# Dividing the attention weights on VectorE instead of GpSimd, in a fused attention + SwiGLU + GELU kernel

## The chip, the cores and the metric

The kernel runs on one core of one Trainium2 chip. The metric is device time in microseconds (us) of one execution; lower is better. Engines are named as the profile names them: PE is TensorE (PEld its weight loads), DVE is VectorE, ACT is ScalarE, POOL is GpSimd (Pool in the prose), SP is the queue that issues the DMAs.

## What is computed

Attention with 4 batches of 8 heads, 576 positions and 64 columns a head, a causal mask and a bias from cumulative sums; then a SwiGLU layer (512 to 1536 to 512) with an RMS norm ahead of it, then a GELU-like layer (512 to 2048 to 512), over 2304 tokens, all in float32:

```python
scores = scale * q @ k.T;  cum = cumsum(maximum(s, 0))
scores = where(causal, -1e9, scores + minimum(-(cum_i - cum_j), 0))
scores = scores - max(scores)
attn = exp(scores)
attn = attn / (sum(attn) + 1e-09)
x = attn @ v
x = swiglu(x / rms(x) * rms_g)
return (h * sigmoid(1.702 * h)) @ w_out,  with h = x @ w_in
```

The change concerns the line that divides by the sum.

## The kernel before, in words

Phase A is the attention, one head after another, 32 in all. The 576 queries of a head are cut into blocks of 64, 128, 128, 128 and 128; under the causal mask these have 64, 192, 320, 448 and 576 keys, so that the weights P of a head are five tiles with 1600 columns together (the first two share one tile, `p01`). For a head, in this order:

- `scores` (L298): PE multiplies into PSUM (L307, or L309 and L310 from head 8 on); DVE adds the mask and takes the row minimum while it copies to SBUF (L323, a custom instruction with an accumulator read behind it).
- `expo` (L329): ACT takes the exponential in place and the row sums SU (L333).
- `recip` (L338): ACT adds 1e-9 to the sums (L340), DVE inverts them into RC (L341), one instruction of five columns a head.
- `norm` (L343): five `tensor_scalar` instructions multiply the five tiles by their column of RC in place (L348). The engine is `en("NORM", ...)`, a letter of a ten-letter string: before, all are `g`, Pool.
- `transp` (L362): PE transposes P into PSUM (L368; the first block of a head L370). In heads 0 to 11 the result is copied out by ACT or DVE (L104, L106); from head 12 on ACT writes a rounded part (L378) and DVE the rest of it (L379, `ptl`).
- `pv` (L397): PE multiplies with V (L416 or L427), ACT and DVE put the result into `xT` (L104; L432, L437).

Ahead of that stands the preparation of q, k and v, which splits a number into a rounded part and its rest (`rnd`, L98 and L100; `rest`, L111 on Pool and L113 on DVE), and in the same stretch the first twelve weight units are decoded from 64-bit floats by `load_unit` (L134): DMA into `wst` (two buffers), then ACT L155, DVE L156, Pool L157, DVE L158 and L160, Pool L162, ACT L98, Pool L164.

From head 13 on the SwiGLU layer's first four column blocks are worked as filler between the heads (`fa_gv`, `fa_act`, `fa_out`: PE L171 and L530, DVE L513, L514 and L113). Phase B (L613, from about 408 us) does the rest of both layers; PE is busy almost throughout there, and no norm lies in it.

The order of the work on each engine is not written out: each call gets a key in heads (`at(key, fn, ...)`, L178; the norms of head h have h + 1.0 to h + 1.08, `recip` h + 0.95), an offset per kind (`off`), and from that a priority. A scheduler with a timeline of its own takes the calls by priority and readiness and fixes one in-order list of instructions for each engine when the kernel is built. P has three buffers a tile (`PPB`), the two PSUM pools for scores and transposes two each.

Of the kernel before, what the change touches and what calls it, by code (L numbers as in the profile page):

```python
# [30 lines left out]
E_MAX = 122880.0 - 2.0 ** -7  # L31


PRM = {'RF': set(), 'QF': {0, 1, 2, 3, 4, 5, 6, 7}, 'VF': {0, 1, 2, 3, 4, 5, 6, 7, 8, 9, 10, 11}, 'DEC0': 7.7, 'DEC1': 12.54, 'DADD': 'ggggggggg', 'DLO': 'ggggvgggg', 'QA': 'ss', 'KA': 'gs', 'VH': 'vg', 'VL': 'gg', 'NORM': 'gggggggggg', 'F0': 13.06, 'F1': 34.62, 'off': {'fa_split': 2.82, 'fa_out': 1.98, 'prep_k': 2.88, 'prep_v32': 0, 'norm': -1.96, 'prep_v': 0.11, 'fa_gv': 0.29, 'prep_load': 0.68, 'prep_f32': 0, 'prep_cum': 0.22, 'scores': -0.04, 'recip': 0, 'transp': -0.26, 'rms_mean': 0, 'load_unit': 0, 'rms_apply': 0, 'expo': 0, 'rms_sq': -1.1, 'pv': 0.19, 'prep_q': 2.7, 'rcast': -0.77}, 'QL': 'gv', 'KL': 'gg', 'PTC': 'ssvv', 'XC': 'ss', 'RMA': 'ggvvgvggvvgv', 'XH': 'sssssvs', 'XL': 'vgggggg', 'HH': 'ssg', 'YO': 'ssssvvs', 'T0': 1.5, 'NX': 7, 'SX': 3, 'TX': 2, 'VX': 2, 'PPB': 3, 'PTB': 5, 'QKB': 2, 'G0': 4, 'XHB': 2, 'VB': 2, 'HHB': 5, 'GA': 4, 'AJ': [0, 1, 2, 3, 4, 5, 6], 'LATE': 1, 'PLB': 4, 'EJ': 2, 'EL': 3}


@with_exitstack
def attention_then_swiglu_then_gelu(ctx: ExitStack, tc, qT, kT, vp, s, w1, w2, gT, out):
# [21 lines left out]
    NIN = len(TIN)  # L60
    GA, G0 = PRM["GA"], PRM["G0"]
    AJ = []
    for t in PRM["AJ"]:
        AJ.append((t, list(range(GA))) if t < 10 else (t - 10, list(range(GA, G0))))
    TA = sum(n for _, n in TIN)
    NW = 3 * G0
    NSLOT = 16
    QF = PRM["QF"]
    VF = PRM["VF"]
    RF = PRM["RF"]  # L70

# [20 lines left out]
    def en(name, i=0):  # L92
        v = PRM[name]
        return ENG[v[i % len(v)]]
# [727 lines left out]
```

## Time and profile before

| | |
|---|---|
| median of 3 runs | 1132.45 us (1128.24 to 1134.29) |
| profiled execution, its own time | 1130.19 us |
| its span, first to last instruction | 1128.4 us |
| mean granted TensorE clock | 0.973 of full speed |
| PE busy | 1087.4 us (96%) |
| DVE busy | 741.9 us (66%) |
| ACT busy | 531.2 us (47%) |
| POOL busy | 443.0 us (39%) |
| the five norms of 32 heads, POOL L348 | 160 instructions, 88.9 us |

Busy is time inside instructions; an instruction that started and then had to wait inside for a port counts as busy, so its length is compared with the shortest of its kind. A page line "idle before, releaser" tells how long an engine had nothing to do before such an instruction, and what ended that. PE's time is that of the whole program; the attention ends about 368 us after the start.

### The profile page before, as it was taken

The page shows a single profiled execution, that of the slowest core. Times are in us where ns is not written, and L with a number is a line of the kernel's source. Part 1 is how long each engine was busy: PE and PEld are TensorE (multiplying, and loading weights), DVE is VectorE, ACT ScalarE, POOL GpSimd, SP SyncE. Part 2 cuts the span into 40 slices and gives each one's busy share as a digit, 9 for nine tenths or more (in the row PEclk, how much of TensorE's full clock was granted, in tenths as well). Part 3 has the DMA queues.
Part 4 walks back from the last instruction along what each step waited for, and adds up shares of the span by engine and source line. Part 5 has one row for each costly group of instructions (what it writes and reads, how often), then busy time and mean ns, then how long its engine had stood idle before and what let it go on. Part 6 is the DMA issues. An engine that isn't in the chain of part 4 may idle for free.

```text
span 1128.4 us, 16751 instructions
## 1 busy us (share of the span) xinstructions
PE 1087.4 (96%) x6000; PEld 943.0 (84%) x6000; DVE 741.9 (66%) x1521; ACT 531.2 (47%) x1210; POOL 443.0 (39%) x496
## 2 busy tenths in 40 slices
PE   6988999999899999999999999999999999999998
PEld 4766898899799889888888888888888888888886
DVE  6668888867976686885954597773335874563433
ACT  4666677767665434543432343443325533343221
POOL 5787977846753234543510352330006530210000
PEclk9987999899899899999999999999999999999999
DMA  4453443223310061221210121120002210000112
GB/s 124 117 170 112 119 130 101 88 75 102 99 32 20 21 205 56 83 87 42 90 38 1 46 86 38 45 68 1 1 1 83 86 57 1 19 1 19 37 38 74
DMA packets 39550, 73.72 MB, mean 65 GB/s; under 512 B 4726, under 2 KB 18038, under 8 KB 39468
## 3 DMA queue, kind: packets, MB, share of 16 engines
q1 hardware_dynamic: 39468, 72.66, 21.3%
q8 instruction: 47, 0.77, 0.3%
q14 instruction: 35, 0.29, 0.1%
HBM read 60.62 MB, written 8.48 MB: 61 GB/s over the span
## 4 chain that ended last, share of the span: by engine, by line
PE 73%; DVE 13%; DMA 5%; POOL 4%; issue 3%; ACT 3%; SPq 1%; DVEq 0%; POOLq 0%; ACTq 0%
PE pg L171 25%; PE py L712 17%; PE py L709 7%; PE pv L171 7%; PE gv L171 6%; DMA wst<-in_w_dram 3%; PE v L427 2%; PE o L530 2%; PE t L368 2%; DVE p L323 2%; DVE xh L113 1%; POOL p L348 1%; DVE wm L156 1%; PE v L416 1%; POOL wa L162 1%
## 5 line engine op out<-in xcount | busy, mean ns | idle before, releaser
L171 PE MATMUL pg<-xh,wu 128*128 128x512 f32 (+2 forms) x1536 | 338.2, 365 | 1.1 <-ACT wu L98 1.0
L171 PEld LDWEIGHTS pg<-xh,wu 128*128 128x128 f32 x1536 | 268.3, 189 | 48.4 <-ACT wu L98 1.1
L712 PE MATMUL py<-wu,hh 128*128 128x512 f32 x864 | 210.1, 389 | 0.0
L164 POOL TENSOR_TENSOR wu<-wa,wu 128x512 fp32r<-128x512 f32 x67 | 91.3, 1363 | 287.9 <-ACT wu L98 287.6
L712 PEld LDWEIGHTS py<-wu,hh 128*128 128x128 f32 x864 | 161.4, 188 | 32.9
L162 POOL TENSOR_TENSOR wa<-wa,wst 128x512 int32<-128x512 int32 x68 | 98.7, 1451 | 123.7 <-DVE wa L160 116.1
L113 DVE SCALAR_TENSOR_TENSOR hh<-u,hh 128x512 fp32r<-128x512 f32 (+2 forms) x128 | 96.1, 751 | 63.3 <-ACT hh L98 63.1
L693 DVE SCALAR_TENSOR_TENSOR u<-th,pg 128x512 f32<-128x512 f32 (+1 forms) x80 | 50.5, 632 | 130.1 <-ACT th L691 129.7
L709 PE MATMUL py<-hh,wu 128*128 128x512 f32 (+2 forms) x576 | 123.4, 357 | 1.5 <-DVE hh L113 1.3
L98 ACT ACTIVATE hh<-u 128x512 fp32r<-128x512 f32 (+2 forms) x128 | 73.7, 576 | 101.3 <-DVE u L685 43.6
L171 PE MATMUL pv<-xh,wu 128*128 128x512 f32 (+2 forms) x576 | 119.5, 356 | 0.0
L709 PEld LDWEIGHTS py<-hh,wu 128*128 128x128 f32 x576 | 98.0, 188 | 17.4 <-DVE hh L113 2.0
L691 ACT ACTIVATE th<-pg 128x512 f32<-128x512 f32 (+1 forms) x80 | 44.2, 554 | 142.8 <-PE pg L171 142.6
L333 ACT ACTIVATE p<-p,MX 128x64 f32<-128x64 f32 (+4 forms) x160 | 88.6, 556 | 48.4 <-DVE MX L323 47.5
L171 PEld LDWEIGHTS pv<-xh,wu 128*128 128x128 f32 x576 | 97.5, 188 | 15.2
L348 POOL TENSOR_SCALAR p<-p,RC 128x64 f32<-128x64 f32 (+4 forms) x160 | 88.9, 575 | 36.9 <-DVE RC L341 35.9
L155 ACT ACTIVATE wst<-wst 128x512 int32<-128x512 uint32 x68 | 46.4, 682 | 109.2 <-DMA wst<-in_w_dram 106.5
L171 PE MATMUL gv<-x,wu 128*128 128x256 f32 (+1 forms) x672 | 96.8, 287 | 0.4 <-DVE th L514 0.2
L171 PEld LDWEIGHTS gv<-x,wu 128*128 128x128 f32 x672 | 88.0, 193 | 1.4 <-DVE th L514 0.9
L368 PE MATMUL t<-ident,p 128*128 128x128 f32 x448 | 76.7, 287 | 5.8 <-ACT pt L104 4.1
L323 DVE CUSTOM_DVE_ANT_0 p<-s,mask 128x64 f32<-128x64 f32 (+4 forms) x160 | 64.5, 422 | 19.9 <-PE s L310 10.4
L368 PEld LDWEIGHTS t<-ident,p 128*128 128x128 f32 x448 | 55.1, 147 | 12.5 <-ACT pt L104 5.9
(101 smaller groups left out, 1677.5 us busy)
## 6 DMA issues: line engine op xcount, KB each, us to landing
wst<-in_w_dram SPq DMA_DIRECT2D x68, 512.0 KB
QS<-in_qT_dram SPq DMA_DIRECT2D x56, 144.0 KB
KS<-in_kT_dram SPq DMA_DIRECT2D x56, 144.0 KB
out_dram<-xT SPq DMA_DIRECT2D x18, 256.0 KB
VS<-in_vp_dram SPq DMA_DIRECT2D x16, 256.0 KB
QB<-QA SPq DMA_DIRECT2D x24, 144.0 KB
y_d<-yo SPq DMA_DIRECT2D x12, 256.0 KB
yb<-y_d SPq DMA_DIRECT2D x6, 512.0 KB
```

The lines of the kernel that those rows point to most:

```text
L98: nc.scalar.activation(out=o, in_=i, func=AF.Copy, scale=c)
L113: eng.scalar_tensor_tensor(out=o, in0=i, scalar=c, in1=hi, op0=ALU.mult, op1=ALU.subtract)
L162: nc.gpsimd.tensor_tensor(out=ai, in0=ai, in1=li, op=ALU.add)
L164: (en("DLO", i) if i < NW else nc.gpsimd).tensor_tensor(out=t[:, 1, :], in0=a, in1=t[:, 0, :], op=ALU.subtract)
L171: nc.tensor.matmul(o, w[:, a, wc:wc + P], x(b, k), start=first and n == 0, stop=last and n == 2,)
L323: nc.vector.tensor_tensor_reduce(out=pt[:m, k0:k0 + n], in0=ps[:m, c0:c0 + n], in1=mask[:m, moff:moff + n], scale=-0.125, scalar=mx[:, 4:5 ...
L333: nc.scalar.activation(out=d["p", qb][:m, :], in_=d["p", qb][:m, :], func=AF.Exp, scale=-1.0, bias=MXt[h % NB][:m, col:col + 1], accum_out ...
L348: eng.tensor_scalar(out=pt[:m, :], in0=pt[:m, :], scalar1=RCt[h % NB][:m, qb:qb + 1], scalar2=1.0, op0=ALU.mult, op1=ALU.mult,)
L368: nc.tensor.transpose(ps[:, c:c + m], d["p", qb][:, Q0[kb]:Q0[kb] + P], ident)
L693: nc.vector.scalar_tensor_tensor(out=u_[:, :n], in0=th[:, :n], scalar=1.0, in1=pg[:, :n], op0=ALU.add, op1=ALU.mult)
L709: nc.tensor.matmul(pss[o][:, :n], w[:, a, o * P:o * P + P], hh[:, b, :n], start=first and m == 0, stop=last and m == 2)
L712: nc.tensor.matmul(pss[o], hh[:, a, o * P:o * P + P], w[:, b, :], start=first and m == 0, stop=last and m == 2)
```

## The change

One string of the table is other: the engine of all five norms of every head is DVE instead of Pool.

```diff
-'NORM': 'gggggggggg'
+'NORM': 'vvvvvvvvvv'
```

Since the scheduler fixes the order anew, the lists of PE, ACT, DVE and Pool all change. Three places:

DVE, around the reciprocal of head 17 (p and RC are the weights and inverted sums, MX the minima, t and pt the transposes; ISA is L323). Before:

```order
L437 TENSOR_TENSOR xT<-v,bt 64x256
L379 TENSOR_TENSOR ptl<-t,pt 128x512
L341 RECIPROCAL RC_134<-RC_134 128x5
L323 ISA p_2168,MX_129<-s,mask 128x320
L323 ISA MX_129 128x1
L323 ISA p_2207,MX_129<-s,mask 128x448
L323 ISA MX_129 128x1
```

Behind the reciprocal DVE went on with the scores of the next head. Now:

```order
L323 ISA p_2168,MX_129<-s,mask 128x320
L323 ISA MX_129 128x1
L341 RECIPROCAL RC_134<-RC_134 128x5
L348 TENSOR_SCALAR p_1951<-p_1951,RC_134 128x64
L348 TENSOR_SCALAR p_1951<-p_1951,RC_134 128x192
L348 TENSOR_SCALAR p_1995<-p_1995,RC_134 128x320
L348 TENSOR_SCALAR p_2024<-p_2024,RC_134 128x448
L348 TENSOR_SCALAR p_2039<-p_2039,RC_134 128x576
L379 TENSOR_TENSOR ptl<-t,pt 128x512
L113 SCALAR_TENSOR_TENSOR hh<-th,hh 128x256
L323 ISA p_2207,MX_129<-s,mask 128x448
L323 ISA MX_129 128x1
```

The five norms stand directly behind the reciprocal; the rest of a transpose, a rest of the filler and the next scores stand behind them.

Pool, at head 9 (KB, QA, KA are prepared keys and queries, wa, wm, wu a weight unit). Before:

```order
L111 TENSOR_TENSOR KB<-KS_119,KA 64x576
L157 TENSOR_SCALAR wm<-wm 128x512
L164 TENSOR_TENSOR wu<-wa,wu 128x512
L100 TENSOR_SCALAR KA<-KS_118 128x576
L348 TENSOR_SCALAR p_907<-p_907,RC_133 128x64
L348 TENSOR_SCALAR p_907<-p_907,RC_133 128x192
L348 TENSOR_SCALAR p_926<-p_926,RC_133 128x320
L348 TENSOR_SCALAR p_960<-p_960,RC_133 128x448
L348 TENSOR_SCALAR p_987<-p_987,RC_133 128x576
L111 TENSOR_TENSOR KB<-KS_118,KA 64x576
```

Now, in that part of the program:

```order
L111 TENSOR_TENSOR KB<-KS_119,KA 64x576
L164 TENSOR_TENSOR wu<-wa,wu 128x512
L157 TENSOR_SCALAR wm<-wm 128x512
L100 TENSOR_SCALAR KA<-KS_118 128x576
L111 TENSOR_TENSOR KB<-KS_118,KA 64x576
L111 TENSOR_TENSOR QA<-QS_116,QA 64x576
```

Pool keeps the splits and its steps of the weight units, in nearly the same order, with no norms between them.

## Rows read from the trace of the kernel before

**Rows 1.** Stages of phase A: length, busy us and instructions by engine, PE clock, DMA

```profile
core 0: us, PE busy (x) PEld busy (x) DVE busy (x) ACT busy (x) POOL busy (x), PEclk, DMA share, GB/s
28.00:84.00 56.00, 49.74 (x267) 40.18 (x265) 35.82 (x100) 36.63 (x103) 44.52 (x53) 0.95 0.51 145
84.00:140.00 56.00, 51.35 (x284) 44.40 (x284) 47.69 (x120) 39.23 (x106) 47.66 (x56) 0.84 0.40 115
140.00:224.00 84.00, 78.39 (x574) 73.00 (x573) 73.19 (x202) 61.45 (x168) 63.07 (x82) 0.92 0.37 107
224.00:364.00 140.00, 135.69 (x1073) 131.22 (x1071) 105.10 (x293) 93.23 (x249) 77.24 (x105) 0.96 0.22 65
sum 336.00, PE 315.16 PEld 288.81 DVE 261.80 ACT 230.54 POOL 232.49; mean PE 78.79 PEld 72.20 DVE 65.45 ACT 57.64 POOL 58.12
```

**Rows 2.** The same view, L348 alone (five instructions a head)

```profile
28.00:84.00 56.00, 17.29 (x30) 0.95 0.51 145
84.00:140.00 56.00, 14.84 (x25) 0.84 0.40 115
140.00:224.00 84.00, 22.45 (x40) 0.92 0.37 107
224.00:364.00 140.00, 26.45 (x50) 0.96 0.22 65
sum 336.00, POOL 81.02; mean POOL 20.26
```

**Rows 3.** Waits between 28 and 364 us: who for whom, us, times, longest

```profile
ACT p L333 <- DVE MX L323: 36.6, 36, 3.9
PEld s L309 <- DVE MX L323: 12.4, 18, 1.7
```

**Rows 4.** The chain of waits between 28 and 364 us, shares by line

```profile
by line: PE gv L171 16.8%; PE v L427 7.5%; PE o L530 7.0%; PE t L368 6.6%; issue 6.4%; DVE p L323 5.7%; DMA wst<-in_w_dram 4.8%; PE v L416 3.5%; POOL p L348 3.2%; PE s L309 3.0%; PE s L310 2.7%; DVE QA L113 2.4%; DVE ptl L379 2.0%; DVE xT L
```

**Rows 5.** Single lines: shortest/median/longest ns, first and last start, shapes

```profile
L158 DVE TENSOR_SCALAR wm<-wm x68: 386/426/1576, 19.0 to 987.1; 128x512 int32<-128x512 int32 x68
L100 DVE TENSOR_SCALAR V<-VS x10: 357/748/1401, 125.9 to 347.9; 128x320 fp32r<-128x320 f32 x10
L100 DVE TENSOR_SCALAR x<-xT x4: 284/570/2006, 298.8 to 303.1; 128x256 fp32r<-128x256 f32 x4
L106 DVE COPY pt<-t x24: 645/684/693, 27.0 to 133.6; 128x512 f32<-128x512 f32 x24
L113 DVE SCALAR_TENSOR_TENSOR hh<-th,hh x24: 405/464/1614, 140.2 to 357.6; 128x256 fp32r<-128x256 f32 x24
L113 DVE SCALAR_TENSOR_TENSOR QA<-QS,QA x12: 755/1205/1932, 72.0 to 325.3; 64x576 fp32r<-64x576 f32 x12
L160 DVE SCALAR_TENSOR_TENSOR wa<-wst,wm x12: 645/725/2210, 31.1 to 162.6; 128x512 int32<-128x512 int32 x12
```

**Rows 6.** DVE groups between 28 and 364 us: busy us, mean ns | idle before

```profile
L113 DVE SCALAR_TENSOR_TENSOR hh<-th,hh 128x256 fp32r<-128x256 f32 x24 | 16.2, 675 | 0.4 <-POOL hh L100 0.3
L113 DVE SCALAR_TENSOR_TENSOR QA<-QS,QA 64x576 fp32r<-64x576 f32 x12 | 14.6, 1217 | 4.6 <-ACT QA L98 4.2
L160 DVE SCALAR_TENSOR_TENSOR wa<-wst,wm 128x512 int32<-128x512 int32 x12 | 11.8, 983 | 2.4 <-POOL wu L164 2.3
L158 DVE TENSOR_SCALAR wm<-wm 128x512 int32<-128x512 int32 x13 | 9.6, 742 | 1.6 <-POOL wm L157 1.6
L100 DVE TENSOR_SCALAR V<-VS 128x320 fp32r<-128x320 f32 x10 | 7.6, 756 | 2.5 <-PE v L427 1.2 <-issue 1.1
```

**Rows 7.** Timeline near 119 us: start us, us, engine, line, operation

```profile
118.47 2.73 POOL L348 TENSOR_SCALAR p<-p,RC 128x64 f32<-128x64 f32 x5
...
119.40 2.77 DVE L113 SCALAR_TENSOR_TENSOR x<-xT,x 128x256 fp32r<-128x256 f32 x1
```

**Rows 8.** Timeline, head 6: its reciprocal and its norms

```profile
64.41 0.19 DVE L341 RECIPROCAL RC<-RC 128x5 f32<-128x5 f32 x1
...
68.81 2.57 POOL L348 TENSOR_SCALAR p<-p,RC 128x64 f32<-128x64 f32 x5
```

**Rows 9.** The slice of 28 us in which DVE was fullest

```profile
280.00:308.00 28.00, 23.93 (x141) 20.76 (x141) 26.66 (x77) 18.87 (x53) 21.80 (x31) 0.82 0.38 110
```

More of the change, by code (lines that the diff above doesn't have):

```diff
@@ L31 @@
 E_MAX = 122880.0 - 2.0 ** -7
-PRM = {'RF': set(), 'QF': {0, 1, 2, 3, 4, 5, 6, 7}, 'VF': {0, 1, 2, 3, 4, 5, 6, 7, 8, 9, 10, 11}, 'DEC0': 7.7, 'DEC1': 12.54, 'DADD': 'ggggggggg', 'DLO': 'ggggvgggg', 'QA': 'ss', 'KA': 'gs', 'VH': 'vg', 'VL': 'gg', 'NORM': 'gggggggggg', 'F0': 13.06, 'F1': 34.62, 'off': {'fa_split': 2.82, 'fa_out': 1.98, 'prep_k': 2.88, 'prep_v32': 0, 'norm': -1.96, 'prep_v': 0.11, 'fa_gv': 0.29, 'prep_load': 0.68, 'prep_f32': 0, 'prep_cum': 0.22, 'scores': -0.04, 'recip': 0, 'transp': -0.26, 'rms_mean': 0, 'load_unit': 0, 'rms_apply': 0, 'expo': 0, 'rms_sq': -1.1, 'pv': 0.19, 'prep_q': 2.7, 'rcast': -0.77}, 'QL': 'gv', 'KL': 'gg', 'PTC': 'ssvv', 'XC': 'ss', 'RMA': 'ggvvgvggvvgv', 'XH': 'sssssvs', 'XL': 'vgggggg', 'HH': 'ssg', 'YO': 'ssssvvs', 'T0': 1.5, 'NX': 7, 'SX': 3, 'TX': 2, 'VX': 2, 'PPB': 3, 'PTB': 5, 'QKB': 2, 'G0': 4, 'XHB': 2, 'VB': 2, 'HHB': 5, 'GA': 4, 'AJ': [0, 1, 2, 3, 4, 5, 6], 'LATE': 1, 'PLB': 4, 'EJ': 2, 'EL': 3}
+PRM = {'RF': set(), 'QF': {0, 1, 2, 3, 4, 5, 6, 7}, 'VF': {0, 1, 2, 3, 4, 5, 6, 7, 8, 9, 10, 11}, 'DEC0': 7.7, 'DEC1': 12.54, 'DADD': 'ggggggggg', 'DLO': 'ggggvgggg', 'QA': 'ss', 'KA': 'gs', 'VH': 'vg', 'VL': 'gg', 'NORM': 'vvvvvvvvvv', 'F0': 13.06, 'F1': 34.62, 'off': {'fa_split': 2.82, 'fa_out': 1.98, 'prep_k': 2.88, 'prep_v32': 0, 'norm': -1.96, 'prep_v': 0.11, 'fa_gv': 0.29, 'prep_load': 0.68, 'prep_f32': 0, 'prep_cum': 0.22, 'scores': -0.04, 'recip': 0, 'transp': -0.26, 'rms_mean': 0, 'load_unit': 0, 'rms_apply': 0, 'expo': 0, 'rms_sq': -1.1, 'pv': 0.19, 'prep_q': 2.7, 'rcast': -0.77}, 'QL': 'gv', 'KL': 'gg', 'PTC': 'ssvv', 'XC': 'ss', 'RMA': 'ggvvgvggvvgv', 'XH': 'sssssvs', 'XL': 'vgggggg', 'HH': 'ssg', 'YO': 'ssssvvs', 'T0': 1.5, 'NX': 7, 'SX': 3, 'TX': 2, 'VX': 2, 'PPB': 3, 'PTB': 5, 'QKB': 2, 'G0': 4, 'XHB': 2, 'VB': 2, 'HHB': 5, 'GA': 4, 'AJ': [0, 1, 2, 3, 4, 5, 6], 'LATE': 1, 'PLB': 4, 'EJ': 2, 'EL': 3}
 @with_exitstack
```

## The prediction

> **What bounds the kernel now.** I read the stages of phase A first, because every norm lies there; phase B has none, and I let it keep its length. Between 28 and 364 us [rows 1] PE is busy 315 of 336 us, and the 21 us that it lacks lie mostly between 28 and 224 us: there the attention sets the pace, while from 224 us on filler keeps PE at 97%. The same rows show the room on the other engines: DVE 64%, 85%, 87% and 75% busy in the four stages, Pool 80%, 85%, 75% and 55%. The reader should see that Pool is the fuller one early, and that DVE has the least room left between 84 and 224 us. Next the waits [rows 3]: ACT stands idle 36.6 us for DVE's minima (L323), and PE's score matmuls wait 12.4 us for them. So DVE's queue feeds both ACT and PE. Last the chain [rows 4]: the norms on Pool hold 3.2% of this stretch, 10.8 us; DVE's score step alone holds 5.7%.
>
> **What is removed from Pool.** In these stages 145 norms of 29 heads, 81.0 us or 2.79 us a head [rows 2]. That is no gain by itself: Pool is not what most others wait for. It counts in two ways, (c) and (d) below.
>
> **(a) What DVE has to do in addition.** The trace has no DVE instruction in float32 with RC as its operand; the nearest are its other `tensor_scalar` instructions from SBUF to SBUF. Undisturbed they take 284 ns for 256 columns and 386 ns for 512 [rows 5], so 0.398 ns a column and 182 ns fixed. For 64, 192, 320, 448 and 576 columns that makes 207, 258, 309, 360 and 411 ns, 1.55 us a head. Ends: 1.2 us if all scaled like the 386 ns without a fixed part (1600 columns); 2.0 us if DVE went as slowly as in its copies out of PSUM, 645 ns for 512 columns (L106). I keep 1.55, since the two rows are the same operation on the same memory. [...]
>
> **(b) The port.** In these stages L158 averages 742 ns against its shortest 386, and V's L100 756 against 357 [rows 5, 6]: about 0.38 us lost in each, while Pool is busy 69% of the time [rows 1]. At 119.40 us [rows 7] a DVE split of 256 columns, a kind whose shortest takes 405 ns (hh in rows 5), took 2.77 us and ended only after Pool's run of five norms, at 121.20. So a `tensor_scalar` of DVE waits when Pool is busy, whatever Pool is doing. Without the norms Pool has 232.5 - 81.0 = 151.5 us, 45%; scaled by that each norm on DVE loses 0.38 x 45/69 = 0.25 us, 1.23 us a head. Ends: 0 if the five, back to back, are never interrupted; 2.0 us if each loses the full 0.40. I take the scaled value, since the rows are this instruction in this stretch. [...]
>
> **(c) What DVE no longer waits for.** Of the kinds in rows 6, mean less shortest [rows 5] times their number is 6.5 (hh), 5.5 (QA), 4.1 (L160), 4.6 (L158) and 4.0 (V), 24.7 us. The norms are 35% of Pool's busy time, so I give them 8.6 us, 0.30 us a head; ends 0 and all of it, 0.85.
>
> **The sum on DVE.** 1.55 + 1.23 - 0.30 = 2.48 us a head. With 6, 5, 8 and 10 heads in the stages [rows 2] DVE comes to 50.7 of 56, 60.1 of 56, 93.0 of 84 and 129.9 of 140 us. The fullest slice before had DVE at 26.66 of 28 us, 95% [rows 9], so I let a stage be no fuller than that. The first and the last stage hide their part in DVE's idle time; if that cover were gone they would cost 14.9 and 24.8 us. The second needs 63.1 us (+7.1), the third 97.7 (+13.7): +20.8 us if each stage keeps its own work. If all of it may shift along the 336 us, 333.7/0.952 = 350.5, +14.5 us. The filler between the heads can move a little and the heads can't; I take the middle, +17.5.
>
> **(d) What the path gains.** A norm batch would be as long as before (1.55 + 1.23 = 2.78 against 2.79 us), so the 10.8 us on the chain don't shrink. What goes is the time in which the norms stood in Pool's queue behind splits and weight steps: in head 6 the reciprocal was there at 64.41 us and the norms began at 68.81 [rows 8], 4.2 us behind its end. Many heads are transposed much later anyway. I give the whole stretch one such wait, -4; ends 0 and -12, three of them. The weight units move past no norm on Pool any more, but wait behind the same norms on DVE (L156, L158, L160): nothing either way. SP's queue keeps its DMAs and their number; they start when buffers come free, which stays with the heads' pace.
>
> **What now stands behind the norms.** On DVE's list the rest of the transpose (L379), for which PE waits, the filler's rest (L113) and the next head's minima (L323), for which ACT waits; a batch of 2.8 us ahead of each is the price already in the sum.
>
> Sum: +17.5 - 4 = +13.5 us on the profiled execution's 1130.2, 1143.7; that execution is 2.3 us under the median, so against 1132.45 I say 1145.
>
> **Rivals.**
> - *Pool's queue set the pace, and the port costs little* (faster). If (b) is 0, a head adds 1.25 us, DVE comes to 298 of 336 us (89%), and the norm batch shrinks from 2.79 to 1.55 us: 4.8 of the 10.8 us on the chain, with two or three of the queue's waits (8 to 12 us) some 13 to 15 us gained, less 2 where DVE's third stage is full: 1120. For it: Pool at 80% and 85% between 28 and 140 us. Against: the 0.38 us lost in each such instruction. It decides where a head adds under 2.0 us to DVE: (0.952 x 336 - 261.8)/29.
> - *Filler takes it up* (no change). PE's work is the same; if the scheduler puts filler wherever a head is late, PE stays as full as now and only the tail shifts: 1132, 5 either way. For it: PE at 97% from 224 us on, with DVE at 75%. Against: before head 13 there is no filler to place, and between 84 and 224 us there is not enough to hide what is missing today.
> - *PE's clock falls too* (slower by more). In the stage where PE was 92% busy the granted clock was 0.84, in the one at 97% it was 0.96 [rows 1]. If the 140 us from 224 on ran at 0.84 as well they would take 160: with the sum above about 1165.
> - That the change doesn't do what it says is excluded: the lists show all norms on DVE.
>
> **How the numbers follow.** The forecast has 0.58, with a range of its own from 1137 to 1158; faster 0.20 (1120), no change 0.13 (1132), clock 0.09 (1165). The bound for no change is 0.5%, 5.7 us, about what a measurement of this kernel can tell: 1126.8 to 1138.1. Faster gets 0.18 (its case without the part that lands inside the bound), the same 0.16 (its case and edges of two others), slower 0.66. The ends of (a) and (b) taken together would reach from a gain of 12 to a loss of over 50 us; I hold them unlikely to meet, and take 1120 to 1166, which leaves out half of the faster case and half of the clock's.
>
> **What would show it.** Right: L348 on DVE, 160 times, 2.3 to 3.2 us a head instead of 1.55; DVE over 90% busy from 84 to 224 us; ACT's wait for L323 longer than 36.6 us; the last norm later than before; L158 and V's L100 still far over their shortest. Wrong: the norms at about 1.5 us a head (the port costs nothing), or the transposes of the last head earlier than before, or phase A as long as before with DVE over 95% (then filler took it up).

## The result, and the profile after

The changed kernel takes 1145.11 us (median of 4 runs, 1143.03 to 1149.71); the kernel before took 1130.35 us beside it (4 runs, 1127.87 to 1134.29). The ratio is 1.0129, with a 95% interval from 1.009 to 1.0168: slower by 14.8 us. The profiled execution took 1144.03 us, its span is 1142.2 us against 1128.4.

The first view is the page's table of engines, after:

```profile
PE 1091.8 (96%) x6000; PEld 943.0 (83%) x6000; DVE 786.3 (69%) x1681; ACT 533.2 (47%) x1210; POOL 354.8 (31%) x336
```

Pool lost 88.2 us, the norms' 88.9. DVE has 160 instructions more but only 44.4 us, 1.39 us a head; the norms themselves take 70.8 us there (below), so DVE's other work holds some 26 us less than before.

Where the 13.8 us of the span arose is seen in the first and last filler matmul, and in the first matmul of phase B (single lines: count, shortest/median/longest ns, first to last start in us). Before:

```profile
L171 PE MATMUL pg<-xh,wu x1536: 274/389/793, 385.7 to 1117.2; 128*128 128x512 f32 x144, 128*128 128x256 f32 x36, 128*128 128x288 f32 x12
...
L171 PE MATMUL gv<-x,wu x672: 250/280/561, 117.7 to 381.2; 128*128 128x256 f32 x144, 128*128 128x192 f32 x24
```

After:

```profile
L171 PE MATMUL pg<-xh,wu x1536: 274/389/794, 400.0 to 1131.4; 128*128 128x512 f32 x144, 128*128 128x256 f32 x36, 128*128 128x288 f32 x12
...
L171 PE MATMUL gv<-x,wu x672: 251/281/553, 128.3 to 395.4; 128*128 128x256 f32 x144, 128*128 128x192 f32 x24
```

The first filler starts 10.6 us later, the last 14.2, phase B 14.3; phase B itself is unchanged (742.2 us from its first matmul to the end of the span, 742.7 before; that first matmul stood at 385.7 us, not at about 408). So it all lies in phase A, three quarters of it ahead of the first filler.

What PE does up to that matmul is the same 2418 matmuls in both kernels. The stages view of that stretch, before and after:

```profile
0.00:385.71 385.71, 351.90 (x2418) 319.77 (x2418) 291.75 (x800) 253.40 (x687) 249.75 (x331) 0.93 0.33 95
0.00:399.96 399.96, 356.19 (x2418) 319.44 (x2418) 335.93 (x960) 255.33 (x687) 161.92 (x171) 0.92 0.31 92
```

PE idles 43.8 us instead of 33.8, and its matmuls take 4.3 us more: the granted clock is at 0.5 of full speed for 62 us of the stretch instead of 52, and at 1.00 for the rest. Of PE's waits over 0.15 us, those that DVE ended come to 30.6 us, 17.1 before; Pool ended none now, and 0.5 us before. So the 14.3 us are 10 of idling, with more waiting for DVE, and 4 of clock.

The stages of phase A, after, as in [rows 1]:

```profile
core 0: us, PE busy (x) PEld busy (x) DVE busy (x) ACT busy (x) POOL busy (x), PEclk, DMA share, GB/s
28.00:84.00 56.00, 48.94 (x264) 37.97 (x262) 49.73 (x139) 39.32 (x109) 31.35 (x27) 1.00 0.48 144
84.00:140.00 56.00, 45.43 (x227) 36.58 (x227) 54.52 (x143) 35.92 (x98) 32.01 (x29) 0.79 0.42 121
140.00:224.00 84.00, 77.66 (x549) 71.57 (x548) 72.78 (x218) 57.07 (x155) 34.00 (x35) 0.90 0.31 90
224.00:364.00 140.00, 134.01 (x1044) 128.97 (x1043) 118.53 (x344) 93.71 (x247) 52.30 (x56) 0.94 0.24 72
sum 336.00, PE 306.05 PEld 275.09 DVE 295.57 ACT 226.01 POOL 149.65; mean PE 76.51 PEld 68.77 DVE 73.89 ACT 56.50 POOL 37.41
```

Between 84 and 140 us DVE is 97% busy and PE, at 92% before, is down to 81%, with a granted clock of 0.79 instead of 0.84. Over the four stages PE works 306 instead of 315 us.

The norms on DVE, one shape to a line (whole program: busy us, mean ns | idle before), then all shapes together, and their shortest, median and longest:

```profile
L348 DVE TENSOR_SCALAR p<-p,RC 128x576 f32<-128x576 f32 x32 | 22.7, 708 | 0.0
L348 DVE TENSOR_SCALAR p<-p,RC 128x448 f32<-128x448 f32 x32 | 18.8, 588 | 0.0
L348 DVE TENSOR_SCALAR p<-p,RC 128x64 f32<-128x64 f32 x32 | 14.9, 466 | 0.4
L348 DVE TENSOR_SCALAR p<-p,RC 128x320 f32<-128x320 f32 x32 | 14.4, 449 | 0.0
...
L348 DVE TENSOR_SCALAR p<-p,RC 128x192 f32<-128x192 f32 x32 | 10.4, 324 | 0.0
...
L348 DVE TENSOR_SCALAR p<-p,RC 128x64 f32<-128x64 f32 (+4 forms) x160 | 70.8, 507 | 0.4
...
L348 DVE TENSOR_SCALAR p<-p,RC x160: 238/383/2682, 19.5 to 377.1; 128x64 f32<-128x64 f32 x32, 128x192 f32<-128x192 f32 x32, 128x320 f32<-128x320 f32 x32, 128x448 f32<-128x448 f32 x32
```

The five shapes make 81.2 us of single durations, 70.8 us once overlapping edges are counted once, 2.21 us a head. A disturbed and an undisturbed batch, from the timeline of DVE:

```profile
102.70 4.41 DVE L348 TENSOR_SCALAR p<-p,RC 128x64 f32<-128x64 f32 x5
...
376.00 1.57 DVE L348 TENSOR_SCALAR p<-p,RC 128x64 f32<-128x64 f32 x5
```

and what Pool did during the first of them:

```profile
102.48 0.76 POOL L100 TENSOR_SCALAR KA<-KS 128x576 fp32r<-128x576 f32 x1 [0.33 <-PE s L309]
103.32 0.66 POOL L157 TENSOR_SCALAR wm<-wm 128x512 f32<-128x512 f32 x1
103.95 1.46 POOL L111 TENSOR_TENSOR KB<-KS,KA 64x576 fp32r<-64x576 f32 x1
105.38 1.41 POOL L164 TENSOR_TENSOR wu<-wa,wu 128x512 fp32r<-128x512 f32 x1
```

Pool runs four instructions almost without a gap until 106.79 us, and DVE's five, 1.57 us by themselves, end at 107.11. They come through one by one: four of the five each wait out one instruction of Pool and end 0.05 to 0.32 us behind it (the last two at 105.67 and 107.11, Pool's at 105.41 and 106.79). 17 of the 32 batches take 1.56 to 1.58 us, 15 take longer. So DVE still waits behind Pool, now with its norms behind what Pool has left. Such waits are all that the traces show of what the prediction and the text ahead of it call the port: in the kernel before, L158 started 28 times while Pool was inside an instruction, and each time ended 278 to 288 ns behind one of Pool's.

The kinds of DVE instructions that waited before [rows 6] are shorter now. The groups of DVE between 28 and 364 us, after:

```profile
L113 DVE SCALAR_TENSOR_TENSOR QA<-QS,QA 64x576 fp32r<-64x576 f32 x12 | 11.6, 968 | 3.2 <-ACT QA L98 2.9
...
L100 DVE TENSOR_SCALAR V<-VS 128x320 fp32r<-128x320 f32 x10 | 4.3, 425 | 0.8 <-PE v L427 0.7
```

They were 1217 and 756 ns. Last the chain of waits between 28 and 364 us, as in [rows 4]:

```profile
by line: PE gv L171 16.2%; DVE p L348 10.1%; PE v L427 8.2%; PE t L368 7.6%; DVE p L323 7.1%; PE o L530 6.0%; PE s L309 4.0%; issue 4.0%; PE s L310 3.2%; PE v L416 3.2%; DMA wst<-in_w_dram 2.6%; DVE ptl L379 2.5%; DVE QA L113 1.8%; DVE wm L
```

The norms were 10.8 us of the chain on Pool; on DVE they are 10.1%, 34 us. The norms end no later behind their reciprocal than before (2.80 us in the mean, 3.64 before); the reciprocals and the minima come later. ACT waits longer for the minima (waits between 28 and 364 us, after), 48.6 us against 36.6 [rows 3]:

```profile
ACT p L333 <- DVE MX L323: 48.6, 49, 3.7
```

### The profile page after: what moved, and what is told of

Same layout as the page of the kernel before. It is cut to its first block, busy times and chain, and to the rows that moved or that the text cites. A ratio compares the mean times of both kernels' runs of the same rounds, so it can differ in the third digit from the quotient of the medians.

```text
span 1142.2 us, 16718 instructions
## 1 busy us (share of the span) xinstructions
PE 1091.8 (96%) x6000; PEld 943.0 (83%) x6000; DVE 786.3 (69%) x1681; ACT 533.2 (47%) x1210; POOL 354.8 (31%) x336
## 4 chain that ended last, share of the span: by engine, by line
PE 76%; DVE 14%; DMA 3%; ACT 2%; issue 2%; POOL 2%; SPq 0%; DVEq 0%; ACTq 0%; POOLq 0%
PE pg L171 25%; PE py L712 17%; PE pv L171 8%; PE py L709 8%; PE gv L171 6%; DVE p L348 3%; PE v L427 3%; PE t L368 3%; DVE p L323 2%; PE o L530 2%; DMA wst<-in_w_dram 2%; DVE xh L113 1%; PE s L309 1%; PE v L416 1%; PE s L310 1%
## 5 line engine op out<-in xcount | busy, mean ns | idle before, releaser
L171 PEld LDWEIGHTS pv<-xh,wu 128*128 128x128 f32 x576 | 97.7, 188 | 15.2
L348 DVE TENSOR_SCALAR p<-p,RC 128x64 f32<-128x64 f32 (+4 forms) x160 | 70.8, 507 | 0.4
L323 DVE CUSTOM_DVE_ANT_0 p<-s,mask 128x64 f32<-128x64 f32 (+4 forms) x160 | 64.3, 421 | 8.1 <-PE s L307 6.3
L368 PEld LDWEIGHTS t<-ident,p 128*128 128x128 f32 x448 | 54.5, 146 | 15.3 <-DVE p L348 5.9
```

Source lines behind the costliest of these rows:

```text
L171: nc.tensor.matmul(o, w[:, a, wc:wc + P], x(b, k), start=first and n == 0, stop=last and n == 2,)
L323: nc.vector.tensor_tensor_reduce(out=pt[:m, k0:k0 + n], in0=ps[:m, c0:c0 + n], in1=mask[:m, moff:moff + n], scale=-0.125, scalar=mx[:, 4:5 ...
L348: eng.tensor_scalar(out=pt[:m, :], in0=pt[:m, :], scalar1=RCt[h % NB][:m, qb:qb + 1], scalar2=1.0, op0=ALU.mult, op1=ALU.mult,)
L368: nc.tensor.transpose(ps[:, c:c + m], d["p", qb][:, Q0[kb]:Q0[kb] + P], ident)
```

## The experiments

Each is compared with runs of the kernel before on the same chip; its median stands between 1131.05 and 1132.29 us in the three sets. Differences below are between these medians, intervals are of the ratio.

**Which heads.** Four kernels move the norms of some heads only; first the early and the late ones.

```diff
-        eng = en("NORM", qb + 5 * (h % 2))
+        eng = nc.vector if h < 13 else nc.gpsimd
```

> The norms of heads 0 to 12 on VectorE, those of heads 13 to 31 on Pool as before. In the changed kernel the reciprocal of head 13 came 8.1 us later than before (152.2 against 144.1 us) and that of head 31 10.7 us later. Theory A (VectorE has no room left between 84 and 140 us, and the loss arises there): some 8 us over before, 1136 to 1142. Rival B (each norm on VectorE costs its share, wherever it stands): 13 of 32 heads, 0.41 x 14.8 = +6, 1136. Rival C (the loss comes in the later stages, where filler and heads compete): within 3 us of before.

Measured 1135.69 against 1131.5 us, ratio 1.0032 (1.0011 to 1.0054): +4.2, Rival B's number; Theory A's and Rival C's ranges just miss it.

```diff
-        eng = en("NORM", qb + 5 * (h % 2))
+        eng = nc.vector if h >= 13 else nc.gpsimd
```

> The norms of heads 0 to 12 on Pool, those of heads 13 to 31 on VectorE. Theory A: the later stages hide most of it, +2 to +4 us, 1132 to 1135. Rival B: 19 of 32 heads, +9, 1139. Rival C: +10 to +14, 1140 to 1145.

Measured 1147.51 against 1131.5 us, ratio 1.015 (1.0127 to 1.0173): +16.0, as much as the whole change and more than any of the three expected. Theory A had the place wrong. The first and last filler of the two, in this order:

```profile
L171 PE MATMUL gv<-x,wu x672: 250/280/582, 134.0 to 388.6; 128*128 128x256 f32 x144, 128*128 128x192 f32 x24
```

```profile
L171 PE MATMUL gv<-x,wu x672: 250/281/582, 116.9 to 396.5; 128*128 128x256 f32 x144, 128*128 128x192 f32 x24
```

With the early heads on DVE the filler starts 16.3 us late and ends 7.4 late: more than half of the delay is made good while the later heads' norms are on Pool. With the late heads on DVE it starts on time and ends 15.3 us late. The profiled execution of the first kernel took 1138.15 us, 2.5 over its median. The two don't add up to the change (20.2 against 14.8 us).

Then the late heads in two groups, by where filler ran out before:

```diff
-        eng = en("NORM", qb + 5 * (h % 2))
+        eng = nc.vector if h in (17, 18, 19, 25, 26, 27) else nc.gpsimd
```

> The norms of six heads alone on VectorE: 17, 18, 19, 25, 26 and 27; all others on Pool. These are the heads around which, in the trace of before, the filler has run out and VectorE is 97 to 99% busy (193.1 to 201.2 us and 287.6 to 304.5 us). Theory F (the loss arises where no filler is left and VectorE sets the pace): most of the 16 us of the kernel with heads 13 to 31 on VectorE, +8 to +14, 1139 to 1145. Rival B (each norm costs its share of those 16 us): 6/19, +5, 1136.

Measured 1143.1 against 1132.29 us, ratio 1.0093 (1.007 to 1.0116): +10.8.

```diff
-        eng = en("NORM", qb + 5 * (h % 2))
+        eng = nc.vector if h in (13, 14, 15, 16, 20, 21, 22, 23, 24, 28, 29, 30, 31) else nc.gpsimd
```

> The other thirteen heads from 13 on (13 to 16, 20 to 24, 28 to 31) have their norms on VectorE, the gap heads and heads 0 to 12 on Pool. Theory F: PE is kept busy by filler there, so -5 to +3 us against before, 1126 to 1134. Rival B: 13/19 of 16, +11, 1142.

Measured 1142.36 against 1132.29 us, ratio 1.0087 (1.0061 to 1.0114): +10.1. A gap head costs 1.8 us in all and a covered one 0.8, but most of that difference does not arise in the gaps. The last filler of the two, gap heads first:

```profile
L171 PE MATMUL gv<-x,wu x672: 250/280/579, 116.6 to 387.5; 128*128 128x256 f32 x144, 128*128 128x192 f32 x24
...
L171 PE MATMUL gv<-x,wu x672: 248/281/553, 118.4 to 392.2; 128*128 128x256 f32 x144, 128*128 128x192 f32 x24
```

Up to there the gap heads have cost 6.3 us (387.5 instead of 381.2), 1.0 a head, and the covered ones 11.0, 0.85 a head. The gap heads' other 4.5 us arise behind the first matmul of phase B; a wait of PE of 1.9 us behind a late weight unit is a part of them, the rest is not traced. So Theory F fails, which had -5 to +3 for the covered heads: by these executions, ahead of phase B, a late norm costs about its share in the gaps and outside them, as Rival B has it. What the gaps are is seen in the kernel before, in stretches between two reciprocals where no filler ran, or almost none (seven matmuls in the third; stages view):

```profile
102.00:116.50 14.50, 12.26 (x51) 9.91 (x51) 14.26 (x44) 11.72 (x33) 13.81 (x17) 0.65 0.44 122
193.10:201.20 8.10, 6.18 (x24) 4.70 (x23) 7.93 (x31) 5.20 (x18) 6.02 (x8) 0.56 0.30 80
287.60:304.50 16.90, 13.87 (x63) 11.58 (x63) 16.50 (x45) 10.07 (x29) 15.04 (x22) 0.70 0.29 82
```

DVE is 98% busy in all three (14.26 of 14.5, 7.93 of 8.1, 16.50 of 16.9 us), PE idles for 15 to 24%, and the granted clock is 0.56 to 0.70. An average of 64 to 87% over a stage hid that. Pool is at 95% and 89% in the first and the third, so that DVE is not the only full engine there; and as the covered heads cost nearly as much, these stretches don't explain the loss.

**What taking the norms off Pool is worth, and what adding them to DVE costs.**

```diff
-        if h not in RF:
-            for qb in range(5):
-                at(h + 1.0 + 0.02 * qb, norm, h, qb)
```

> Leaves the division out altogether: no norm on any engine, P goes undivided into the transposes. It shows what taking the norms off Pool is worth with nothing added on VectorE. Theory A (Pool's norms were hidden but for the 10.8 us that they hold on the chain): 5 to 12 us under before, 1118 to 1125. Rival D (Pool's queue and its hold of the port set the pace before): 15 us or more under before, under 1115. If it is within 3 us of before, the change could not have gained anything whatever VectorE did.

Measured 1113.19 against 1131.5 us, ratio 0.9849 (0.9826 to 0.9872): -18.3. So the norms on Pool were not hidden, and Rival D's number is the one that came. The stretch up to the first matmul of phase B there, as above:

```profile
0.00:365.80 365.80, 339.95 (x2418) 313.10 (x2418) 278.40 (x800) 252.23 (x687) 161.50 (x171) 0.95 0.35 100
```

PE idles 25.9 us instead of 33.8, its waits for DVE are 9.7 us instead of 17.1, and the same matmuls take 12.0 us less, with the clock at 0.5 for 34 us instead of 52. DVE, which lost no work, is busy 12.4 us less (729.5 against 741.9): the same 1521 instructions take less time. Read with the change, the trade was some 18 us gained by taking the norms from Pool and off the path, and 33 us (14.8 + 18.3) paid for 56.8 us more on DVE. Only the kernel without norms also takes them off the path, so the 18 us are a ceiling, and the 33 too.

```diff
             op0=ALU.mult, op1=ALU.mult,
         )
+        n = pt.shape[1]
+        nc.vector.tensor_scalar(
+            out=mask[:m, :n], in0=mask[:m, :n], scalar1=RCt[h % NB][:m, qb:qb + 1], scalar2=1.0,
+            op0=ALU.min, op1=ALU.mult,
+        )
```

> The norms stay on Pool, and VectorE gets five more instructions of the same widths and kind, with RC as operand, on the constant mask (its values stay as they are): VectorE's load is added without anything taken off Pool or off the path from the reciprocal to the transposes. Theory A (VectorE's time is the cost): as slow as the change or slower, 1143 to 1155, since Pool's norms now meet these at the port. Rival E (the cost is that the norms on the path to the transposes now stand in VectorE's queue and wait for the port there): within 5 us of before.

Measured 1158.29 against 1131.5 us, ratio 1.0247 (1.022 to 1.0274): +26.8. No tile waits for these instructions but DVE's own, Pool keeps its work, and it is worse than the change and than Theory A's range: Rival E falls, time added to DVE costs without any norm of the path standing in its queue. It is not DVE's time alone, though. Pool's norms take 96.6 us there instead of 88.9, and PE waits 9.4 us for them instead of 0.5; how much of that is the longer norms and how much a late reciprocal is not parted. Its page:

```profile
PE 1096.0 (95%) x6000; PEld 945.7 (82%) x6000; DVE 804.7 (70%) x1681; ACT 532.0 (46%) x1210; POOL 450.4 (39%) x496
```

DVE has 62.8 us more than before.

**Waits behind Pool, or DVE's time.** Here the division has another form of the instruction; that this form would not wait for Pool was the author's guess, which no trace had shown.

```diff
-            out=pt[:m, :], in0=pt[:m, :], scalar1=RCt[h % NB][:m, qb:qb + 1], scalar2=1.0,
-            op0=ALU.mult, op1=ALU.mult,
+            out=pt[:m, :], in0=pt[:m, :], scalar1=RCt[h % NB][:m, qb:qb + 1], scalar2=0.0,
+            op0=ALU.mult, op1=ALU.add, accum_out=junk[:m, qb:qb + 1],
```

> The change, with the division in the form of the instruction that also writes an accumulator (an unused sum). [...] Theory P (the port's wait and the long batches of up to 4.4 us made the loss): 1132 to 1140. Theory L (VectorE's time is what costs, waiting or working): slower than the change by up to 8 us, 1145 to 1153. If the longest norm is far over the shortest, the form does not avoid the port.

Measured 1153.2 against 1132.29 us, ratio 1.0177 (1.0152 to 1.0202): +20.9. The line of the norm there, and its widest shape:

```profile
L349 DVE TENSOR_SCALAR_CACHE_REDUCE p<-p,RC x160: 261/541/810, 19.0 to 385.3; 128x64 f32<-128x64 f32 x32, 128x192 f32<-128x192 f32 x32, 128x320 f32<-128x320 f32 x32, 128x448 f32<-128x448 f32 x32
```

```profile
L349 DVE TENSOR_SCALAR_CACHE_REDUCE p<-p,RC 128x576 f32<-128x576 f32 x32 | 25.8, 806 | 0.0
...
L349 DVE TENSOR_SCALAR_CACHE_REDUCE p<-p,RC 128x64 f32<-128x64 f32 (+4 forms) x160 | 77.2, 540 | 0.5
```

The widest takes 806 ns in the mean and the longest of all 810: no wait is seen among the 160 norms, where the change had one of 2682 ns (64 columns). The norms take 77.2 us, 2.4 a head, and the accumulator reads 13.0; DVE's time is 805.2 us of the whole program against 786.3, and the kernel is slower. So the loss needs no wait of a norm behind Pool: it comes as well, and larger, where DVE works all that time. Whether the length of a batch counts this run doesn't say, since all but one are 2.4 us long.

```diff
-'NORM': 'vvvvvvvvvv', ... 'norm': -1.96
+'NORM': 'vvvvvvvvvv', ... 'norm': 0.0
```

> The change, with the norms' offset at 0.0 instead of -1.96 heads, so that the scheduler lets other VectorE work that is ready go between the five norms (a rest of a transpose, for instance) instead of behind all five. Theory Q (the place directly behind the reciprocal costs, because transposes' rests and minima stand behind 1.6 to 4.4 us of norms): 4 to 10 us under the change, 1135 to 1141. Theory L: within 4 us of the change, 1141 to 1149.

Measured 1147.46 against 1132.29 us, ratio 1.0137 (1.0112 to 1.0163): +15.2, the change again, and not the gain that Theory Q wants. It is a weak test: in the trace other DVE work stands between the five norms in 6 of the 32 batches, in 1 under the change.

**DVE relieved elsewhere; and the order by itself.** Under the change, Pool gets other work of DVE (the four roundings of the first filler tile go to ACT):

```diff
-'DLO': 'ggggvgggg', ... 'VH': 'vg', ... 'QL': 'gv', ... 'RMA': 'ggvvgvggvvgv', 'XH': 'sssssvs', 'XL': 'vgggggg'
+'DLO': 'ggggggggg', ... 'VH': 'gg', ... 'QL': 'gg', ... 'RMA': 'gggggggggggg', 'XH': 'sssssss', 'XL': 'ggggggg'
```

> The change, and in return Pool takes the preparation work that VectorE shared with it: all rests of q, all roundings of v, all sums of squares, the rest and rounding of the first filler tile, the one decode step of VectorE. By the trace of the changed kernel that is 11.6 us (QA), 4.3 us (V), 3.8 us (SQ), 5.4 us (x) and 0.7 us (wu), 26 us of VectorE's time. Theory L (over the runs so far, each us of VectorE's time in phase A has lengthened it by 0.33 to 0.40 us): 8 to 10 us under the change, 1135 to 1137. Theory S (the lists of the kernel before were tuned to its durations, and any new order costs about 10 us): no nearer to before than the change, 1142 to 1150.

Measured 1141.33 against 1131.05 us, ratio 1.0099 (1.0076 to 1.0122): +10.3, some 4 us better than the change; both theories miss it. DVE came down to 775.0 us, by 11.3 and not by 26. The norms did not pay for that (69.7 us, 70.8 under the change); other DVE work that stayed became longer, L156 of the weight units from 46.1 to 51.2 us and hh from 12.5 to 15.1, beside more work on Pool. 4 us for 11.3 would fit Theory L's rate, but is no more than a new order alone can make (below).

```diff
-'scores': -0.04
+'scores': 0.02
```

> The kernel before with another order and no other work: the offset of the score steps is 0.02 instead of -0.04 heads; 1274 lines of PE's list and 934 of VectorE's stand differently. Norms on Pool. Theory S: +6 to +16 us against before. Theory L: the same VectorE time, so within 5 us of before.

Measured 1131.83 against 1131.05 us, ratio 1.0004 (0.9989 to 1.0018): no difference.

```diff
-'pv': 0.19
+'pv': 0.25
```

> The kernel before with another order and no other work: the offset of the products with V is 0.25 instead of 0.19 heads; 2089 lines of PE's list and 1224 of VectorE's stand differently. Norms on Pool. Theory S: +6 to +16 us against before. Theory L: within 5 us of before.

Measured 1135.07 against 1131.05 us, ratio 1.0032 (1.0014 to 1.005): +4.0. So a new order of some thousand lines cost 0 and 4 us in these two cases, not 14; as far as two orders can tell, Theory S falls, and 4 us is the noise against which the finer differences above have to be read.

```diff
-'RF': set()
+'RF': set(range(12, 32))
```

> A way without norms for heads 12 to 31, which the kernel has in it unused: PE transposes the inverted sums, broadcast over 64 columns, and VectorE multiplies the product with V by them (two instructions a piece and three pieces a head, where it had one and two). It takes 2.79 us a head off Pool, about 0.4 us of port waits off VectorE, and adds four VectorE instructions of about 0.42 us and five PE transposes a head. Theory L: VectorE's net +1.3 us a head over 20 heads, 26 us, times 0.33 to 0.40, +9 to +10, less what Pool's norms cost on the path (a part of the 18 us that leaving them all out gave): 1128 to 1138.

Measured 1152.86 against 1131.05 us, ratio 1.0198 (1.0178 to 1.0219): +21.8, a miss. Its page:

```profile
PE 1106.6 (96%) x6260; PEld 962.1 (84%) x6260; DVE 749.4 (65%) x1601; ACT 535.3 (47%) x1230; POOL 389.6 (34%) x396
```

DVE rose by 7.5 us only; PE got 260 instructions (13 a head: the five transposes and eight more for the product with V) and 19.2 us more, which I had left unpriced, and in the later stages PE was at 97% before. Up to phase B PE idles 33.3 us there, as before (33.8), so the loss is PE's own work. No version beat the kernel before, except the one that leaves the division out.

## Why the prediction was right, and by what steps

The time came as forecast, 1145.1 against 1145 (+14.8 us on the kernel beside it, where +12.6 was forecast), in the direction and the place argued: phase A, DVE fullest between 84 and 140 us, phase B untouched. The mechanism is right in kind: DVE gets more time than it is spared, and PE waits for DVE. That the number fits so closely is luck: the sum on DVE was too high, and the rule that turned it into the kernel's time gave too little for it.

- (a), the work itself, came out, 1.55 us a head against 1.57 for an undisturbed batch, but by two errors that cancel. In the batch at 376.00 us the five norms take 255, 314, 378, 446 and 510 ns, 1.90 us in all and 0.5 ns a column where 0.40 was reckoned; the batch is shorter since each starts some 80 ns before the end of the one ahead.
- (b), the waits behind Pool, was too high: 1.23 us a head against 2.21 - 1.57 = 0.64. I scaled a loss per instruction as if each of the five met Pool afresh. 28 of the 160 norms waited, in 15 of the 32 batches; a batch that met Pool lost 1.4 us, the others nothing.
- (c), the relief, was 0.30; the kernel without norms shows 12.4 / 32 = 0.39, so this was nearly right for what taking the norms off Pool spares DVE. In the change 2.21 - 1.39 = 0.82 us a head are gone from DVE's other work. What is over 0.39 comes only with the norms on DVE and the order that goes with them; no run parts it.
- The sum on DVE is therefore 1.39 us a head and not 2.48. The step that failed is the next one, "let a stage be no fuller than 95%": with 1.39 it gives 47.7 + 7.0 = 54.7 and 73.2 + 11.1 = 84.3 us, at 95.2% 57.5 and 88.6, +6 us in all if each stage keeps its work, nothing if it may shift, +3 in the middle. Less 4 for (d) that is no change, where 14 were measured. DVE's time costs below that bound too, and the second stage went over it (97%).
- No fixed rate takes the rule's place. The change costs 14.8 us for 44.4 us more on DVE (0.33), the kernel whose norms show no wait 20.9 for 63.3 (0.33), the double load 26.8 for 62.8 (0.43); but the late heads alone 16.0 for 26.8 (0.60) and the early ones 4.2 for 16.0 (0.26). All but the double load have a relief on Pool in them.
- (d), the path's gain, I put at 4 us, 12 at the most. Leaving the norms out gave 18.3; how much of it is Pool's queue, the waits between Pool and DVE or the path no run here parts.
- The rival that Pool set the pace had more in it than its 0.20 says: Pool's norms cost up to 18 us. (Its terms, 4.8 and 8 to 12 us, make 13 to 17, not 13 to 15.) Its deciding point, under 2.0 us a head on DVE, was wrong: the change lies under it, at 1.39, and is slower.
- Filler did not take it up: the covered heads alone cost 10.1 us. The clock's rival didn't come in full: the granted clock in the last stage is 0.94, not 0.84, and the clock's part is 4 us.

Of the signs named ahead, DVE at 91% between 84 and 224 us, ACT's longer wait, the later last norm (377.1 us, 367.3 before) and L158 (557 ns against 386) came; the norms' 2.21 us a head lie just under the 2.3 to 3.2, and V's L100, at 425 ns, is not far over its 357 any more.

What stays open is why DVE's time costs what it does at 64 to 87% busy, and why the parts don't add: 4.2 and 16.0 us for early and late heads against 14.8 for both, 10.8 and 10.1 for the two late groups against 16.0. Ahead of phase B the late groups do nearly add (6.3 and 11.0 against 15.3). An early delay seems to be made good where a later one would else arise, but no run shows how.

## What to carry to other kernels

Moving work from Pool to VectorE does not end VectorE's waits behind Pool when the moved instruction waits there as well, as 28 of the 160 norms did here: what counts is the time that VectorE gains in all, its own waits and those that it is spared included. Don't take room for granted because an engine is at 64 to 87% on average: here it was at 98% in some stretches, and added time cost nearly as much outside them. And test both halves by themselves, the work taken away and the work added: here one was worth up to 18 us and the other cost more. A forecast that fits can still have wrong terms; only such runs show them.

## What the runs showed that I had not expected

A norm on VectorE that waited did so mostly for one instruction of Pool, also where Pool had more queued. Of the 28 that waited under the change, 27 were held behind a single instruction of Pool, and ended a time behind it that goes with the width: about 0.05 us for 64 columns, 0.18 for 320, 0.25 for 448, 0.32 for 576. One, of 2682 ns, waited out three. So a batch of 1.57 us took 4.41 beside four of Pool's. The split with two inputs of [rows 7] was held longer: it ended at 122.17 us, behind four of Pool's instructions and not only the norms. The same division in the form with an accumulator showed no wait (806 ns in the mean for 576 columns, 810 the longest of all), but took 90.2 us, reads included, against 70.8.
